# Four late modulation rows of a fused block: three of them summed in float32 on VectorE, one left as matrix-vector products on TensorE

## The chip, the cores and the metric

The kernel runs on one core of a Trainium2 chip. The metric is the device time of one execution in microseconds (us), the median of several runs. A core has TensorE (PE in the profile, with its weight loads as PEld), VectorE (DVE), ScalarE (ACT), GpSimd (POOL) and SyncE (SP), which here only starts transfers. In the profile, L12 is line 12 of the kernel.

## The reference

One transformer block with adaptive layer norm. A vector `c` gives six modulation rows of 1024 numbers; each scales, shifts or gates a part of the block.

```python
x = A_x                                            # (1, 2048, 1024), bfloat16
mod = (silu(c) @ w_mod).reshape(1, 6, 1, 1024)     # w_mod: 1024 x 6144
sa, ca, ga, sb, cb, gb = ...                       # the six rows
h = layernorm(x) * (1 + ca) + sa
x = x + ga * linear_attention(h, A_wqkv, A_wo)     # 32 heads of 32, phi(q), phi(k)
h = layernorm(x) * (1 + cb) + sb
x = x + gb * ((silu(h @ w_gate) * (h @ w_up)) @ w_down)   # 3584 hidden columns
```

`sa` and `ca` are needed at once. `ga`, `sb`, `cb` and `gb` are the four late rows that the change is about: `ga` multiplies the output weights `wo`, `sb` and `cb` shift and scale the second normalized rows, and `gb` gates the last output.

## The kernel before

The 2048 rows are worked in four chunks of 512 (`sc` 0 to 3). Of each chunk come the K groups, the V groups and the products K transposed times V; then the Q groups, numerators and denominators (`nd`), output products (`o`), the gate and up products (`GU`) and the down products (`D`). A group is eight matmuls into one of five PSUM banks that are used in turn. A list `seq` holds the matmul groups in order, and `put(label, ...)` hangs further work behind a group: each engine sees its instructions in exactly that order. Label ("V", 1, 3) is the fourth V group of chunk 1 ("V1.3" in the text).

The late rows as they are computed before: a block of 128 columns of `w_mod` is the stationary operand and one column of silu(c), `scT`, the moving one. So each result is a row turned onto the partitions, one number for each; eight products, one for each eighth of the 1024 inputs, add up in PSUM.

```python
LATE = [(2, "ga"), (3, "sb"), (4, "cb"), (5, "gb")]

def load_late(i):                      # half a row's columns of w_mod: 1 MB
    q, kb = LATE[i // 2][0], i % 2
    k0 = q * D + kb * NB
    nc.sync.dma_start(out=wml[i % 3], in_=wm_v[:, :, k0:k0 + NB])

def late_mm(i):                        # 32 products with one moving column
    ...
    for ii in range(NB // P):
        col = kb * (NB // P) + ii
        for j in range(DC):
            nc.tensor.matmul(mps[:, col:col + 1], lhsT=wml[i % 3][:, j, ii * P:(ii + 1) * P],
                             rhs=scT[:, j:j + 1], start=False, stop=(j == DC - 1), ...)
    if kb == 1:
        nc.vector.tensor_copy(out=m1[:, q, :], in_=mps[:, 0:DC])
```

`sb` and `cb` are used in that form (one number for each partition). `ga` and `gb` are needed along the free axis and alike on all partitions, so they are spread and transposed:

```python
def late_fin(q):
    ...                                # sb: copy; cb: add 1
        nc.vector.tensor_copy(out=rep[:], in_=m1[:, q, :].unsqueeze(2).to_broadcast([P, DC, P]))

def late_bc(q, dst):
    for h in range(NH):
        b = nextbank()
        for i in range(NB // P):
            cc = h * (NB // P) + i
            nc.tensor.matmul(b[:, i * P:(i + 1) * P], lhsT=rep[:, cc, :], rhs=ident[:], ...)
        nc.scalar.copy(out=dst[:, h * NB:(h + 1) * NB], in_=b[:])
```

The work of VectorE beside them in these stages: a K or Q group is evacuated by ScalarE (exp) and two VectorE operations, a V group by ScalarE alone. Behind every second K group stands the layer norm of 128 rows of the next chunk (`ln`): statistics on VectorE, then a power and two more operations on GpSimd, then a DMA transpose. In V4 and V6 of the stage the transposed rows are modulated on VectorE (`modulate`), and the next chunk's K groups need them.

```python
def phi_to(dst, acc):
    nc.scalar.activation(out=e[:], in_=acc, func=ACT.Exp)
    nc.vector.tensor_scalar(out=e[:], in0=e[:], scalar1=1.0, scalar2=PHI_EPS, op0=ALU.min, op1=ALU.add)
    nc.vector.scalar_tensor_tensor(out=dst, in0=acc, scalar=0.0, in1=e[:], op0=ALU.max, op1=ALU.add)

def modulate(sc_, cc, sT, c1T, c0=0, c1=SCW):
    h = M4[:, sc_, cc, c0:c1]
    nc.vector.tensor_scalar(out=h, in0=h, scalar1=c1T[:, cc:cc + 1], scalar2=sT[:, cc:cc + 1], ...)
```

The places of the late work before:

```python
put(("V", 0, 6), lambda: load_late(0), lambda: load_late(1), lambda: load_late(2))
lab = [(k, sc, i) for sc in (1, 2) for k in ("K", "V") for i in (2, 6)]
for i in range(8):
    put(lab[i], lambda i=i: late_mm(i))
    if i + 3 < 8:
        put(lab[i], lambda i=i: load_late(i + 3))
put(("K", 1, 7), lambda: late_fin(2))
put(("V", 1, 1), lambda: late_bc(2, ga_bc))
put(("V", 1, 7), lambda: late_fin(3))
put(("K", 2, 0), lambda: nc.sync.dma_start(out=wo, in_=wo_v))
put(("K", 2, 7), lambda: late_fin(4))
put(("V", 2, 7), lambda: late_fin(5))
put(("K", 3, 1), lambda: late_bc(5, gb_bc))
for cc in range(DC):
    put(("V", 3, cc), lambda cc=cc: nc.vector.tensor_tensor(out=wo[:, cc, :], in0=wo[:, cc, :], in1=ga_bc[:], ...))
```

At the start PE runs 21 products of a zero tile (`warm`) until the first normalized rows are there.

Of the kernel before, what the change touches and what calls it, by code (L numbers as in the profile page):

```python
# [9 lines left out]
ALU = mybir.AluOpType  # L10
BF16 = mybir.dt.bfloat16
F32 = mybir.dt.float32  # L12
# [9 lines left out]
def kernel(  # L22
# [13 lines left out]
    nc = tc.nc  # L36
    P = nc.NUM_PARTITIONS
    _, S, D = A_x.shape
# [3 lines left out]
    DC = D // P  # L42
# [5 lines left out]
    NB = 512  # L48
    NH = D // NB
# [13 lines left out]
    wo_v = A_wo.rearrange("(c p) n -> p c n", p=P)  # L63
# [3 lines left out]
    wm_v = w_mod.rearrange("(p j) n -> p j n", j=DC)  # L67
    c_v = c.rearrange("o (p j) -> p (o j)", j=DC)

    const = ctx.enter_context(tc.tile_pool(name="const", bufs=1))  # L70
# [6 lines left out]
    bank = [psum.tile([P, NB], F32, name=f"bank{i}") for i in range(8)]  # L77
# [3 lines left out]
    M3 = const.tile([P, 16384], BF16, name="M3")  # L81
    M4 = const.tile([P, NSC, DC, SCW], BF16, name="M4")
    M5 = const.tile([P, 14336], BF16, name="M5")
# [3 lines left out]
    def view(region, off, shape, dtype=BF16):  # L87
        n = 1
        for s_ in shape:
            n *= s_  # L90
        w = n * (2 if dtype == F32 else 1)
        ap = region[:, off:off + w]
        if dtype == F32:
            ap = ap.bitcast(F32)
        if len(shape) == 2:
            ap = ap.rearrange("p (a b) -> p a b", a=shape[0])
        elif len(shape) == 3:
            ap = ap.rearrange("p (a b c) -> p a b c", a=shape[0], b=shape[1])
        return ap
# [8 lines left out]
    wml = [view(M3, 4096 * (1 + i), [DC, NB]) for i in range(3)]  # L108
# [9 lines left out]
    wo = view(M6, 0, [DC, D])  # L118
    x1rs = [view(M6, 2048 * i, [D], F32) for i in range(2)]
    obs = [view(M6, 4096 + 1024 * i, [D]) for i in range(2)]  # L120
    yts = [view(M6, 6144 + 1024 * i, [NB], F32) for i in range(2)]
    xs = [view(M7, 1024 * i, [D]) for i in range(6)]
    xns = [view(M7, 6144 + 1024 * i, [D]) for i in range(6)]
    wgs = [view(M7, 4096 * i, [DC, FBW]) for i in range(3)]
# [11 lines left out]
    def load_x(st):  # L136
        nc.sync.dma_start(out=xs[st % 6], in_=x2[st * P:(st + 1) * P, :])
# [22 lines left out]
    load_wk(6, 7)  # L160
    load_wk(7, 8)

    zt = const.tile([P, NB], BF16, name="zt")
    nc.vector.memset(zt[:], 0.0)
    ident = const.tile([P, P], BF16, name="ident")
    make_identity(nc, ident[:])
    neg_half = const.tile([P, 1], F32, name="neg_half")
# [6 lines left out]
    sbT = const.tile([P, DC], BF16, name="sbT")  # L174
    cb1T = const.tile([P, DC], BF16, name="cb1T")
    m1 = const.tile([P, 6, DC], BF16, name="m1")
    ga_bc = const.tile([P, D], BF16, name="ga_bc")
    gb_bc = const.tile([P, D], BF16, name="gb_bc")
    KVZ = const.tile([P, HG, KVW], BF16, name="KVZ")
    rep = const.tile([P, DC, P], BF16, name="rep")  # L180

    scT = const.tile([P, DC], BF16, name="scT")
    nc.scalar.activation(out=scT[:], in_=c_sb[:], func=ACT.Silu)

    def warm(n):
        for _ in range(n):
            nc.tensor.matmul(bank[7][:], lhsT=zt[:, 0:P], rhs=zt[:], start=True, stop=True)


    stat = {}  # L190
# [39 lines left out]
    def nextbank():  # L230
        b = bank[state["b"]]
        state["b"] = (state["b"] + 1) % 5
        return b
# [51 lines left out]
                                    in1=mask[:, P:KVW].unsqueeze(1).to_broadcast([P, n, HPC]), op=ALU.mult)  # L285


    LATE = [(2, "ga"), (3, "sb"), (4, "cb"), (5, "gb")]

    def load_late(i):  # L290
        q, kb = LATE[i // 2][0], i % 2
        k0 = q * D + kb * NB
        nc.sync.dma_start(out=wml[i % 3], in_=wm_v[:, :, k0:k0 + NB])

    def late_mm(i):
        q, kb = LATE[i // 2][0], i % 2
        mps = bank[7][:, 320 + 8 * q:328 + 8 * q]
        for ii in range(NB // P):
            col = kb * (NB // P) + ii
            for j in range(DC):  # L300
                nc.tensor.matmul(mps[:, col:col + 1], lhsT=wml[i % 3][:, j, ii * P:(ii + 1) * P],  # L301
                                 rhs=scT[:, j:j + 1], start=False, stop=(j == DC - 1), skip_group_check=True)
        if kb == 1:
            nc.vector.tensor_copy(out=m1[:, q, :], in_=mps[:, 0:DC])

    def late_fin(q):
        if q == 3:
            nc.vector.tensor_copy(out=sbT[:], in_=m1[:, 3, :])
        elif q == 4:
            nc.vector.tensor_scalar_add(out=cb1T[:], in0=m1[:, 4, :], scalar1=1.0)  # L310
        else:
            nc.vector.tensor_copy(out=rep[:], in_=m1[:, q, :].unsqueeze(2).to_broadcast([P, DC, P]))

    def late_bc(q, dst):
        for h in range(NH):
            b = nextbank()
            for i in range(NB // P):
                cc = h * (NB // P) + i
                nc.tensor.matmul(b[:, i * P:(i + 1) * P], lhsT=rep[:, cc, :], rhs=ident[:], start=True, stop=True)
            nc.scalar.copy(out=dst[:, h * NB:(h + 1) * NB], in_=b[:])  # L320


    def tr0(st):
# [25 lines left out]
    def mod_pair(p):  # L349
        mod_mm(0, 2 * p, 2 * p + 2)  # L350
        mod_mm(1, 2 * p, 2 * p + 2)
        mod_rows(2 * p, 2 * p + 2)

    warm(21)
    for st in range(STC):
        ln_stats(st)
    mask = const.tile([P, KVW], BF16, name="mask")
# [6 lines left out]
    ln_xn(0, False)  # L364
    tr0(0)
    warm(3)
    ln_xn(1, False)
    tr0(1)
# [56 lines left out]
    def put(label, *fns):  # L425
        after.setdefault(label, []).extend(fns)
# [154 lines left out]
    for sc in (2, 3):  # L581
        put_ln(sc, [("K", sc - 1, 1), ("K", sc - 1, 3), ("K", sc - 1, 5), ("K", sc - 1, 7),
                    ("V", sc - 1, 4), ("V", sc - 1, 6)])
    put(("V", 0, 6), lambda: load_late(0), lambda: load_late(1), lambda: load_late(2))
    put(("V", 0, 7), lambda: [load_x(st) for st in range(8, 12)])
    put(("V", 1, 7), lambda: [load_x(st) for st in range(12, 16)])


    lab = [(k, sc, i) for sc in (1, 2) for k in ("K", "V") for i in (2, 6)]
    for i in range(8):  # L590
        put(lab[i], lambda i=i: late_mm(i))
        if i + 3 < 8:
            put(lab[i], lambda i=i: load_late(i + 3))
    put(("K", 1, 7), lambda: late_fin(2))
    put(("V", 1, 1), lambda: late_bc(2, ga_bc))
    put(("V", 1, 7), lambda: late_fin(3))
    put(("K", 2, 0), lambda: nc.sync.dma_start(out=wo, in_=wo_v))
    put(("K", 2, 7), lambda: late_fin(4))
    put(("V", 2, 7), lambda: late_fin(5))
    put(("K", 3, 1), lambda: late_bc(5, gb_bc))  # L600
    for cc in range(DC):
        put(("V", 3, cc), lambda cc=cc: nc.vector.tensor_tensor(out=wo[:, cc, :], in0=wo[:, cc, :], in1=ga_bc[:],
                                                               op=ALU.mult))


    put(("KV", 3, 1), kvz_build)
# [77 lines left out]
```

## Time and profile before

| | |
|---|---|
| device time, median of 3 runs | 847.81 us (846.98 to 849.0) |
| span of the profiled execution | 845.9 us |
| matrix-vector products of the late rows (L301) | 256, from 66.2 to 124.5 us |
| transposing products of the two broadcasts (L319) | 16, first 81.2, last 131.9 us |
| loads of late w_mod columns (L293) | 8 of 1 MB, median 7.4 us from issue to landing |
| load of `wo` (L597) | 1 of 2 MB, issued at 95.2 us, 12.7 us to landing |
| DMA transposes of the first norm (L220) | 12, 3.0 to 6.7 us to landing, median 3.2 |

A group line of the profile reads: source line, engine, operation, output <- inputs, shapes, count | busy us in total, mean ns of one | idle time of the engine just ahead of them, and what ended most of it. A timeline line reads: start in us, duration in us, engine, source line, operation, count, and in brackets the idle time ahead and its releaser. Matmuls are pipelined, so their durations overlap and differences of starts tell what a stream of them costs. The slices of the page divide the span into 40 equal parts of 21.1 us, each digit a tenth of busy time.

### The profile page before, as it was taken

How to read it: one execution, taken by the hardware profiler on the slowest of the kernel's cores; microseconds unless marked ns; L12 is line 12 of the kernel's file. 1: busy time of each engine (PE TensorE's matmuls, PEld its weight loads, DVE VectorE, ACT ScalarE, POOL GpSimd, SP SyncE). 2: the span in 40 equal slices, each digit the busy share in tenths (PEclk: the TensorE clock that was granted, in tenths of full speed). 3: DMA queues.
4: the chain of work that ended last, by engine and by line, in shares of the span. 5: the costliest groups of instructions: out<-in, count | busy, mean ns of one | idle time of the engine just before them, and what ended most of it. 6: DMA issues, size and time to landing. Idle time of an engine off the chain costs nothing.

```text
span 845.9 us, 10893 instructions
## 1 busy us (share of the span) xinstructions
PE 833.4 (99%) x4368; PEld 395.7 (47%) x4452; DVE 322.9 (38%) x617; ACT 144.8 (17%) x270; POOL 78.8 (9%) x142
## 2 busy tenths in 40 slices
PE   8999999999999999999999999999999999999998
PEld 4454554544444444444444444444444444444444
DVE  5667455488755655421111222211122122112222
ACT  4333223322211111111110001111000111100000
POOL 2124130013122323100000000000000000000000
PEclk9999999999999999999999999999999999999999
DMA  9995982056489888778875215555322555201220
GB/s 290 307 242 132 273 196 56 1 125 159 95 220 228 209 220 212 187 227 259 246 232 176 69 60 163 150 150 149 106 75 70 154 154 158 82 18 63 76 69 26
DMA packets 203763, 128.65 MB, mean 152 GB/s; under 512 B 50496, under 2 KB 189888, under 8 KB 203712
## 3 DMA queue, kind: packets, MB, share of 16 engines
q1 hardware_dynamic: 162864, 98.58, 41.0%
q10 hardware_dynamic: 38544, 20.98, 11.2%
q0 software_dynamic: 2304, 8.39, 2.6%
q8 instruction: 35, 0.57, 0.3%
q14 instruction: 16, 0.13, 0.0%
HBM read 103.81 MB, written 12.58 MB: 138 GB/s over the span
## 4 chain that ended last, share of the span: by engine, by line
PE 95%; DVE 1%; SPq 1%; DMA 1%; issue 1%; ACT 0%; DVEq 0%
PE bank L511 23%; PE bank L530 23%; PE bank L505 23%; PE bank L462 7%; PE bank L265 6%; PE bank L257 6%; PE bank L242 5%; DMA M<-in_w_mod_dram 1%; PE bank L435 1%; PE bank L274 1%; PE bank L301 1%; SPq L145 1%; SPq L142 1%; DVE stats L196 0%; DVE M L239 0%
## 5 line engine op out<-in xcount | busy, mean ns | idle before, releaser
L511 PE MATMUL bank<-M,M 128*128 128x512 bf16 x881 | 210.4, 379 | 0.8
L505 PE MATMUL bank<-M,M 128*128 128x512 bf16 x871 | 209.7, 379 | 1.3
L513 DVE TENSOR_TENSOR M<-bank,e 128x512 bf16<-128x512 f32 x112 | 77.4, 691 | 275.1 <-PE bank L511 265.7
L530 PE MATMUL bank<-M,M 128*128 128x512 bf16 (+1 forms) x687 | 146.9, 370 | 0.6
L508 ACT ACTIVATE e<-bank 128x512 f32<-128x512 f32 x112 | 66.8, 597 | 439.7 <-PE bank L505 415.7
L530 PEld LDWEIGHTS <-M 128*128 128x128 bf16 x924 | 90.4, 98 | 103.3
L511 PEld LDWEIGHTS <-M 128*128 128x128 bf16 x896 | 87.7, 98 | 105.7
L505 PEld LDWEIGHTS <-M 128*128 128x128 bf16 x896 | 87.3, 98 | 103.8
L534 DVE TENSOR_TENSOR M<-bank,gb_bc 128x512 f32<-128x512 f32 (+1 forms) x33 | 22.3, 675 | 149.2 <-PE bank L530 135.3
L242 PE MATMUL bank<-M,M 128*128 128x512 bf16 x244 | 57.3, 379 | 1.6 <-DVE M L224 0.6
L462 PE MATMUL bank<-M,M 128*128 128x512 bf16 x254 | 57.8, 379 | 0.1
L265 PE MATMUL bank<-M,M 128*128 128x512 bf16 x250 | 56.7, 379 | 0.3
L257 PE MATMUL bank<-M,M 128*128 128x512 bf16 x250 | 56.2, 379 | 0.3
L237 ACT ACTIVATE e<-bank 128x512 f32<-128x512 f32 x64 | 37.8, 598 | 101.9 <-PE bank L265 48.4
L530 PE MATMUL bank<-M 128*128 128x512 bf16 x219 | 50.7, 379 | 0.3
L239 DVE SCALAR_TENSOR_TENSOR M<-bank,e 128x512 bf16<-128x512 f32 x64 | 44.3, 692 | 3.7
L238 DVE TENSOR_SCALAR e<-e 128x512 f32<-128x512 f32 x64 | 27.7, 433 | 40.5 <-ACT e L237 40.5
L462 PEld LDWEIGHTS <-M 128*128 128x128 bf16 x256 | 25.0, 98 | 29.7
L257 PEld LDWEIGHTS <-M 128*128 128x128 bf16 x256 | 24.7, 98 | 29.0
L265 PEld LDWEIGHTS <-M 128*128 128x128 bf16 x256 | 24.6, 98 | 27.8
L242 PEld LDWEIGHTS <-M 128*128 128x128 bf16 x256 | 24.0, 97 | 28.8 <-DVE M L224 2.1
L464 DVE TENSOR_TENSOR M<-bank,M 128x512 f32<-128x512 f32 x32 | 22.1, 690 | 14.5 <-PE bank L462 14.3
(66 smaller groups left out, 334.1 us busy)
## 6 DMA issues: line engine op xcount, KB each, us to landing
M<-in_B_w_gate_dram SPq DMA_DIRECT2D x56, 512.0 KB, 3.9
M<-in_B_w_up_dram SPq DMA_DIRECT2D x56, 512.0 KB, 5.0
M<-in_w_mod_dram SPq DMA_DIRECT2D x8, 1024.0 KB, 7.4
x_scratch<-M POOLq DMA_DIRECT2D x16, 512.0 KB, 5.6
M<-x_scratch ACTq DMA_DIRECT2D x16, 512.0 KB, 3.4
M<-in_B_w_down_dram SPq DMA_DIRECT2D x6, 1024.0 KB, 7.9
M<-in_A_x_dram SPq DMA_DIRECT2D x16, 256.0 KB, 6.6
M<-in_w_mod_dram SPq DMA_DIRECT2D x8, 512.0 KB, 8.1
```

What stands on the lines that cost most here:

```text
L237: nc.scalar.activation(out=e[:], in_=acc, func=ACT.Exp)
L238: nc.vector.tensor_scalar(out=e[:], in0=e[:], scalar1=1.0, scalar2=PHI_EPS, op0=ALU.min, op1=ALU.add)
L239: nc.vector.scalar_tensor_tensor(out=dst, in0=acc, scalar=0.0, in1=e[:], op0=ALU.max, op1=ALU.add)
L242: nc.tensor.matmul(acc[:], lhsT=M4[:, sc_, cc, t * P:(t + 1) * P], rhs=wk[:, cc, h * NB:(h + 1) * NB], start=(cc == 0), stop=(cc == DC - 1))
L257: nc.tensor.matmul(acc[:], lhsT=M4[:, sc_, cc, t * P:(t + 1) * P], rhs=wv[:, cc, h * NB:(h + 1) * NB], start=(cc == 0), stop=(cc == DC - 1))
L265: nc.tensor.matmul(acc[:], lhsT=wq[:, cc, qc * P:(qc + 1) * P], rhs=M4[:, sc_, cc, :], start=(cc == 0), stop=(cc == DC - 1))
L462: nc.tensor.matmul(acc[:], lhsT=oTs[st % 3][:, cc, :], rhs=wo[:, cc, hs], start=(cc == 0), stop=(cc == DC - 1))
L505: nc.tensor.matmul(g_ps[:], lhsT=wg_blk[:, cc, fs], rhs=M4[:, sc_, cc, :], start=(cc == 0), stop=(cc == DC - 1))
L508: nc.scalar.activation(out=sg[:], in_=g_ps[:], func=ACT.Silu)
L511: nc.tensor.matmul(u_ps[:], lhsT=wu_blk[:, cc, fs], rhs=M4[:, sc_, cc, :], start=(cc == 0), stop=(cc == DC - 1))
L513: nc.vector.tensor_tensor(out=gus[sc_][:, f, :], in0=u_ps[:], in1=sg[:], op=ALU.mult)
L530: nc.tensor.matmul(y_ps[:, 0:w], lhsT=gus[sc_][:, f, t * P:(t + 1) * P], rhs=wd(f)[:, c0:c1], start=(f == 0), stop=(f == FC - 1))
```

## The change

Three of the four late rows leave the matrix-vector form. Each partition holds eight rows of `w_mod`; VectorE multiplies them with the partition's eight values of silu(c) and adds them in float32, which leaves 128 partial rows. A product with ones on PE adds the 128 partitions: with a matrix of ones as the stationary operand the sum comes out alike on all partitions (`ga`, `gb`), with the partial row as the stationary operand and one column of ones as the moving one it comes out turned onto the partitions (`sb`). [...]the float32 sum is split into a high part and a rest, and both are multiplied. `cb` stays in the matrix-vector form. The aim is to take matrix-vector products from TensorE and to use VectorE where it idles; `sb` and `gb` are computed later than before (`gb` in the second chunk's gate and up stage), and the multiplication of `wo` by `ga` moves from the V groups of the last chunk to its K groups.

```diff
+    accA = view(M5, 8256, [D], F32)
+    hlA = [view(M5, 10304 + 1024 * i, [2, NB]) for i in range(2)]
+    accG = view(M3, 12288, [D], F32)
+    hlG = view(M3, 14336, [2, NB])
 ...
-    zt = const.tile([P, NB], BF16, name="zt")
+    zt = view(M5, 13376, [NB])
-    rep = const.tile([P, DC, P], BF16, name="rep")
+    ones = const.tile([P, P], BF16, name="ones")
+    nc.gpsimd.memset(ones[:], 1.0)
+    scF = const.tile([P, DC], F32, name="scF")
 ...
+    nc.scalar.copy(out=scF[:], in_=scT[:])
 ...
+    def late_sum(acc, kb, slot, js):
+        dst = acc[:, kb * NB:(kb + 1) * NB]
+        for j in js:
+            if j == 0:
+                nc.vector.tensor_scalar_mul(out=dst, in0=wml[slot][:, 0, :], scalar1=scF[:, 0:1])
+            else:
+                nc.vector.scalar_tensor_tensor(out=dst, in0=wml[slot][:, j, :], scalar=scF[:, j:j + 1], in1=dst,
+                                         op0=ALU.mult, op1=ALU.add)
+
+    def late_split(acc, kb, hl):
+        src = acc[:, kb * NB:(kb + 1) * NB]
+        nc.vector.tensor_copy(out=hl[:, 0, :], in_=src)
+        nc.vector.tensor_tensor(out=hl[:, 1, :], in0=src, in1=hl[:, 0, :], op=ALU.subtract)
+
+    def late_cols(q, kb, hl):
+        o = 320 + 8 * q
+        for ii in range(NB // P):
+            col = o + kb * (NB // P) + ii
+            for s_ in range(2):
+                nc.tensor.matmul(bank[7][:, col:col + 1], lhsT=hl[:, s_, ii * P:(ii + 1) * P], rhs=ones[:, 0:1], ...)
+
+    def late_vec(q, kb, slot):          # as late_mm before, for cb
 ...
-    def late_bc(q, dst):
-        for h in range(NH):
-            b = nextbank()
-            for i in range(NB // P):
-                cc = h * (NB // P) + i
-                nc.tensor.matmul(b[:, i * P:(i + 1) * P], lhsT=rep[:, cc, :], rhs=ident[:], start=True, stop=True)
-            nc.scalar.copy(out=dst[:, h * NB:(h + 1) * NB], in_=b[:])
+    def late_bc(kb, hl, dst):
+        b = nextbank()
+        for s_ in range(2):
+            nc.tensor.matmul(b[:], lhsT=ones[:], rhs=hl[:, s_, :], start=(s_ == 0), stop=(s_ == 1))
+        nc.scalar.copy(out=dst[:, kb * NB:(kb + 1) * NB], in_=b[:])
 ...
-    warm(21)
+    warm(17)
 ...
+    def sums(acc, kb, slot, labels):
+        for i, lab in enumerate(labels):
+            put(lab, lambda i=i: late_sum(acc, kb, slot, (2 * i, 2 * i + 1)))
+
+    put(("V", 0, 6), lambda: load_late(CB, 0, 0), lambda: load_late(CB, 1, 1), lambda: load_late(GA, 0, 2))
+    put(("K", 1, 2), lambda: late_vec(CB, 0, 0), lambda: load_late(GA, 1, 0))
+    put(("K", 1, 6), lambda: late_vec(CB, 1, 1), lambda: load_late(SB, 0, 1))
+    put(("V", 1, 7), lambda: late_fin(CB))
+    sums(accA, 0, 2, [("V", 1, k) for k in range(4)])
+    put(("V", 1, 3), lambda: late_split(accA, 0, hlA[0]), lambda: load_late(SB, 1, 2))
+    put(("K", 2, 2), lambda: late_bc(0, hlA[0], ga_bc))
+    put(("K", 2, 3), lambda: nc.sync.dma_start(out=wo, in_=wo_v))
+    sums(accA, 1, 0, [("V", 2, k) for k in range(4)])
+    put(("V", 2, 3), lambda: late_split(accA, 1, hlA[1]))
+    put(("K", 3, 0), lambda: late_bc(1, hlA[1], ga_bc))
+    for kb in range(2):
+        sums(accA, kb, 1 + kb, [("V", 3, 4 * kb + k) for k in range(4)])
+    put(("V", 3, 4), lambda: late_split(accA, 0, hlA[0]))
+    put(("KV", 3, 0), lambda: late_split(accA, 1, hlA[1]))
+    put(("Q", 1, 2), lambda: late_cols(SB, 0, hlA[0]), lambda: late_cols(SB, 1, hlA[1]), lambda: late_fin(SB))
+    put(("GU", 0, 20), lambda: load_late(GB, 0, 0), lambda: load_late(GB, 1, 1))
+    for kb in range(2):
+        sums(accG, kb, kb, [("GU", 1, 5 * kb + i) for i in range(4)])
+        put(("GU", 1, 5 * kb + 4), lambda kb=kb: late_split(accG, kb, hlG))
+        put(("GU", 1, 5 * kb + 6), lambda kb=kb: late_bc(kb, hlG, gb_bc))
     for cc in range(DC):
-        put(("V", 3, cc), lambda cc=cc: nc.vector.tensor_tensor(out=wo[:, cc, :], in0=wo[:, cc, :], in1=ga_bc[:], ...))
+        put(("K", 3, 2 + cc) if cc < 6 else ("V", 3, cc - 6), lambda cc=cc: ...)    # the same product
```

The sums of V1.0 and on are hung behind V groups, so they stand in VectorE's order behind the last layer norm of the K stage and ahead of the modulation.

More of the change, by code (lines that the diff above doesn't have):

```diff
@@ L161 @@
     load_wk(7, 8)
-    zt = const.tile([P, NB], BF16, name="zt")
-    nc.vector.memset(zt[:], 0.0)
+    zt = view(M5, 13376, [NB])
+    nc.vector.memset(zt, 0.0)
     ident = const.tile([P, P], BF16, name="ident")
@@ L179 @@
     KVZ = const.tile([P, HG, KVW], BF16, name="KVZ")
-    rep = const.tile([P, DC, P], BF16, name="rep")
+    ones = const.tile([P, P], BF16, name="ones")
+    nc.gpsimd.memset(ones[:], 1.0)
+    scF = const.tile([P, DC], F32, name="scF")
     scT = const.tile([P, DC], BF16, name="scT")
     nc.scalar.activation(out=scT[:], in_=c_sb[:], func=ACT.Silu)
+    nc.scalar.copy(out=scF[:], in_=scT[:])
     def warm(n):
         for _ in range(n):
-            nc.tensor.matmul(bank[7][:], lhsT=zt[:, 0:P], rhs=zt[:], start=True, stop=True)
+            nc.tensor.matmul(bank[7][:], lhsT=zt[:, 0:P], rhs=zt, start=True, stop=True)
     stat = {}
@@ L285, in kvz_build, with load_late @@
                                     in1=mask[:, P:KVW].unsqueeze(1).to_broadcast([P, n, HPC]), op=ALU.mult)
-    LATE = [(2, "ga"), (3, "sb"), (4, "cb"), (5, "gb")]
-    def load_late(i):
-        q, kb = LATE[i // 2][0], i % 2
+    GA, SB, CB, GB = 2, 3, 4, 5
+    def load_late(q, kb, slot):
         k0 = q * D + kb * NB
-        nc.sync.dma_start(out=wml[i % 3], in_=wm_v[:, :, k0:k0 + NB])
-    def late_mm(i):
-        q, kb = LATE[i // 2][0], i % 2
-        mps = bank[7][:, 320 + 8 * q:328 + 8 * q]
[L298 to L310, printed above, removed]
-        else:
-            nc.vector.tensor_copy(out=rep[:], in_=m1[:, q, :].unsqueeze(2).to_broadcast([P, DC, P]))
-    def late_bc(q, dst):
-        for h in range(NH):
-            b = nextbank()
-            for i in range(NB // P):
-                cc = h * (NB // P) + i
-                nc.tensor.matmul(b[:, i * P:(i + 1) * P], lhsT=rep[:, cc, :], rhs=ident[:], start=True, stop=True)
-            nc.scalar.copy(out=dst[:, h * NB:(h + 1) * NB], in_=b[:])
+        nc.sync.dma_start(out=wml[slot], in_=wm_v[:, :, k0:k0 + NB])
@@ new lines, in late_cols @@
+    def late_cols(q, kb, hl):
[3 more added lines that the diff above has]
+            for s_ in range(2):
+                nc.tensor.matmul(bank[7][:, col:col + 1], lhsT=hl[:, s_, ii * P:(ii + 1) * P], rhs=ones[:, 0:1],
+                                 start=False, stop=(s_ == 1), skip_group_check=True)
+    def late_vec(q, kb, slot):
+        o = 320 + 8 * q
+        for ii in range(NB // P):
+            col = o + kb * (NB // P) + ii
+            for j in range(DC):
+                nc.tensor.matmul(bank[7][:, col:col + 1], lhsT=wml[slot][:, j, ii * P:(ii + 1) * P],
+                                 rhs=scT[:, j:j + 1], start=False, stop=(j == DC - 1), skip_group_check=True)
@@ new lines, in late_fin @@
+    def late_fin(q):
+        mps = bank[7][:, 320 + 8 * q:328 + 8 * q]
+        if q == SB:
+            nc.vector.tensor_copy(out=sbT[:], in_=mps)
+        else:
+            nc.vector.tensor_copy(out=m1[:, q, :], in_=mps)
+            nc.vector.tensor_scalar_add(out=cb1T[:], in0=m1[:, q, :], scalar1=1.0)
+    def late_bc(kb, hl, dst):
[3 more added lines that the diff above has]
+        nc.scalar.copy(out=dst[:, kb * NB:(kb + 1) * NB], in_=b[:])
@@ L583 @@
                     ("V", sc - 1, 4), ("V", sc - 1, 6)])
-    put(("V", 0, 6), lambda: load_late(0), lambda: load_late(1), lambda: load_late(2))
     put(("V", 0, 7), lambda: [load_x(st) for st in range(8, 12)])
     put(("V", 1, 7), lambda: [load_x(st) for st in range(12, 16)])
[L589 to L600, printed above, removed]
+    def sums(acc, kb, slot, labels):
+        for i, lab in enumerate(labels):
+            put(lab, lambda i=i: late_sum(acc, kb, slot, (2 * i, 2 * i + 1)))
+    put(("V", 0, 6), lambda: load_late(CB, 0, 0), lambda: load_late(CB, 1, 1), lambda: load_late(GA, 0, 2))
@@ L601 @@
+    for kb in range(2):
+        sums(accG, kb, kb, [("GU", 1, 5 * kb + i) for i in range(4)])
+        put(("GU", 1, 5 * kb + 4), lambda kb=kb: late_split(accG, kb, hlG))
+        put(("GU", 1, 5 * kb + 6), lambda kb=kb: late_bc(kb, hlG, gb_bc))
     for cc in range(DC):
-        put(("V", 3, cc), lambda cc=cc: nc.vector.tensor_tensor(out=wo[:, cc, :], in0=wo[:, cc, :], in1=ga_bc[:],
-                                                               op=ALU.mult))
+        put(("K", 3, 2 + cc) if cc < 6 else ("V", 3, cc - 6),
+            lambda cc=cc: nc.vector.tensor_tensor(out=wo[:, cc, :], in0=wo[:, cc, :], in1=ga_bc[:], op=ALU.mult))
```

## The prediction

> **What bounds the kernel now.** I read the page's busy shares first, then its slices.
>
> ```profile
> PE 833.4 (99%) x4368; PEld 395.7 (47%) x4452; DVE 322.9 (38%) x617; ACT 144.8 (17%) x270; POOL 78.8 (9%) x142
> ...
> PE   8999999999999999999999999999999999999998
> ...
> DVE  5667455488755655421111222211122122112222
> ```
>
> TensorE (PE) is busy in every slice, and the chain of work that ended last is 95% PE. So the time falls only where PE has fewer instructions, or where PE waited. VectorE (DVE) is the engine with room, though not in slices 5 to 12 (about 65 to 190 us), which is where most of the new work goes. Next, the groups by shape: what the change removes (L301, L319) and what resembles the work it adds to VectorE.
>
> ```profile
> L239 DVE SCALAR_TENSOR_TENSOR M<-bank,e 128x512 bf16<-128x512 f32 x64 | 44.3, 692 | 3.7
> ...
> L238 DVE TENSOR_SCALAR e<-e 128x512 f32<-128x512 f32 x64 | 27.7, 433 | 40.5 <-ACT e L237 40.5
> ...
> L301 PE MATMUL bank<-scT,M 128*128 128x1 bf16 x256 | 7.5, 163 | 0.1
> ...
> L319 PE MATMUL bank<-ident,rep 128*128 128x128 bf16 x16 | 1.2, 220 | 1.0 <-DVE rep L312 1.0
> ```
>
> The mean of 163 ns is the latency of one, not what it costs in a pipelined stream. For the cost I take differences of starts in PE's timeline around the first broadcast:
>
> ```profile
> 76.62 3.62 PE L257 MATMUL bank<-M,M 128*128 128x512 bf16 x16
> 81.22 0.62 PE L319 MATMUL bank<-ident,rep 128*128 128x128 bf16 x8 [0.98 <-DVE rep L312]
> 81.68 1.89 PE L257 MATMUL bank<-M,M 128*128 128x512 bf16 x8
> 83.41 0.94 PE L301 MATMUL bank<-scT,M 128*128 128x1 bf16 x32
> 84.21 7.07 PE L257 MATMUL bank<-M,M 128*128 128x512 bf16 x31
> ```
>
> Eight 512-wide products take 83.41 - 81.68 = 1.73 us, 0.216 each. A block of 32 matrix-vector products takes 84.21 - 83.41 = 0.80 us, 25 ns each. Eight transposing products of the broadcast take 81.68 - 81.22 = 0.46 us. The sixteen products from 76.62 should have ended issuing at 76.62 + 16 x 0.216 = 80.07, so PE stood 1.15 us for `rep`. Last, where VectorE idles in the K and V stages:
>
> ```profile
> 80.48 0.68 DVE L312 COPY rep<-m 128x1024 bf16<-128x1024 bf16 x1
> 90.06 2.67 DVE L224 TENSOR_SCALAR M<-M,ca1T,saT 128x512 bf16<-128x512 bf16 x8 [8.89 <-DMA M<-M]
> ...
> 114.73 0.16 DVE L310 TENSOR_SCALAR cb1T<-m 128x8 bf16<-128x8 bf16 x1
> 120.41 2.68 DVE L224 TENSOR_SCALAR M<-M,ca1T,saT 128x512 bf16<-128x512 bf16 x8 [5.52 <-DMA M<-M]
> ...
> 144.26 4.89 DVE L602 TENSOR_TENSOR M<-M,ga_bc 128x1024 bf16<-128x1024 bf16 x8
> 159.63 0.43 DVE L238 TENSOR_SCALAR e<-e 128x512 f32<-128x512 f32 x1 [10.48 <-ACT e L237]
> ```
>
> The holes are 8.89 us in V1, 5.52 us in V2 and 10.48 us in V3. The first two end when the transposed rows of the next chunk land, and then the modulation (L224) must run, because PE needs it at once for K2 and K3.
>
> **What the Trainium skill says.** "TensorE: Matmul & The Clock Gate", section "Wait — 56ns, not 53.3ns?", gives a floor of about 25 ns between starts however narrow the product, and 215.7 ns for 512 columns; the trace agrees (25 and 216). "VectorE: DVE Perf Modes", section "The TRN2 errata", has (N+151)/0.96 for a float32 sum of two tensors, 691 ns at N=512; the trace shows 690 to 692 for L464, L513 and L535. "SBUF — State Buffer", section "SBUF: two separate sides", says that a VectorE operation with two SBUF inputs and a GpSimd operation that reads SBUF lock each other out for a whole instruction. The kernel before has few such pairs; a trace of something like it is the GpSimd power at 80.65, which took 0.92 us beside the copy to `rep` where its median is about 0.6.
>
> **The change part by part: TensorE.**
> - Removed: six of eight late blocks, 6 x 0.80 = 4.8 us. Only `cb` keeps its two.
> - Removed: both transposing broadcasts, 2 x 0.46 = 0.9 us, and the first one's wait, 1.15 us (the second shows none).
> - Added: 16 one-column products for `sb`, 16 x 0.025 = 0.4 us.
> - Added: four broadcasts with ones, two 512-wide products each, 8 x 0.216 = 1.73 us.
> - Sum: -4.8 - 0.9 - 1.15 + 0.4 + 1.73 = -4.7 us.
> - The four warm-up products less (some 0.9 us at the end of the warm-up) I count as nothing. The transposes that follow wait for ScalarE's normalized rows, and PE later waits for w_mod to land at 19.5 and 21.3 us, which does not move.
>
> **VectorE.** Each half row is one scaling (0.43, as L238), seven dependent multiply-adds (0.69 each), a copy (0.43, my guess of the form) and a subtraction (0.69). A dependent instruction starts 0.03 us after its forerunner's end (L238 at 60.31 for 0.43, L239 at 60.77), so a half row takes 0.46 + 7 x 0.72 + 0.46 + 0.69 = 6.65 us, and six of them 40 us. They displace nothing if they lie in holes:
> - V1: the work of K1 ends at 80.5, the sums at 87.1, before the 90.06 at which the modulation started: free.
> - V2: PE has gained by then and reaches K2 3.2 us earlier (1.15 + 0.46 + two blocks), so VectorE ends its K2 work at about 111.3 and the sums at 118.0. The modulation then takes 2.7 us, to 120.7.
> - V3: the products of `wo` move into K3 (0.61 us each beside 1.07 for the evacuation of a group, under 1.73 of PE), two remaining; 13.3 + 1.2 us of work in the 15.4 us that were the old products plus the hole. Just free.
> - The `gb` row: 2 multiply-adds in each 3.46 us of the up and gate stage, where VectorE is a fifth busy: free. Its 2 MB load comes at some 328 us, eight column steps of 3.46 us before it is used.
>
> **Rivals, and what each would make of the time.**
> - A new wait of PE at the start of K2 and K3 replaces part of the gain. PE would be at K3 at 127.19 - 3.2 - 3.2 (four blocks) + 0.43 = 121.2 us and need the eighth modulated piece 1.5 us later, at 122.7. The last rows leave GpSimd at 117.11 - 3.5 = 113.6, or about 1.3 later if its three operations are each held by a multiply-add with two SBUF inputs. The transposes land 3.2 us (median) to 6.7 us (longest) after issue, and the 2 MB of `wo`, now loaded in K2 instead of ahead of it, can make it the longer one: 118 to 121.6, the modulation ends at 120.8 to 124.3, PE waits 0 to 1.6 us. At K2 the same sum gives 0 to 0.8. For it: the locks and the displaced `wo` load. Against it: the late w_mod load that competed with the transposes at 84.6 us now comes after the sums. I take 0.15 at K2 and 0.6 at K3. At its worst: 845.5 us.
> - VectorE becomes the bound in V3, late for the K,V mask and the first numerators. For it: the hole is filled to within 1 us. Against it: PE reads the masked product 2.6 us after VectorE made it, and five rotating banks carry evacuations. Cost up to 1 us; 844.8 at most with the first rival as taken.
> - The gain was hidden anyway, PE meeting a DMA later. Against it: after 22 us PE has no DMA wait in its groups. This would give 847; I do not believe it.
> - The `gb` load delays weights of the next blocks. Between 325 and 345 us the DMA moved about 190 GB/s where it reaches 380 elsewhere, and weights are issued some 19 us ahead. Near zero.
>
> **The range and the chances.** 847.81 - 4.7 + 0.75 = 843.86, given as 843.8 us. The three runs before lie 2 us apart, so the median of a few runs is good to about 1 us. With no new wait it is 843.1, less 1 for scatter: 842.0. With the worst waits and scatter: 846.0. 2% are 17 us, more than the whole of what is removed or added on PE, so both outer chances are 0.01.
>
> **What would show each step.** PE's busy time falls by 3.5 to 4 us, and the blocks of 32 occur twice, not eight times, in K1. The wait of PE on `rep` is gone. Multiply-adds read near 690 ns, and the six half rows near 6.7 us each. The VectorE holes in V1, V2 and V3 shrink to under 3 us; those in GU stay. A PE idle on L224 ahead of K2 or K3 sizes the first rival. I am wrong if multiply-adds are much slower beside GpSimd, if a PE wait above 2 us appears in the K, V or Q stages, or if PE waits for weights after 328 us.

## The result and the profile after

| | before | after |
|---|---|---|
| device time, median | 847.47 us (846.98 to 849.0, 4 runs) | 842.53 us (842.26 to 842.78, 4 runs) |
| span of the profiled execution | 845.9 us | 840.4 us |

The ratio is 0.9939, with a 95% interval of 0.9921 to 0.9956: 4.9 us less. Both medians are of few runs. In the comparisons of the experiments below the kernel before has 847.24 to 847.33 us (9 to 27 runs), and the kernel after, run again, 842.74 us: about 4.6 us less. In the kernel after, L250 are the K groups, L265 the V groups, L282 the products K transposed times V, L329 the products left to `cb`, L343 the broadcasts with ones, L321 the one-column products for `sb`, L306 and L308 the scaling and the multiply-adds of the sums, L313 and L314 the split, L232 the modulation.

First the busy shares and VectorE's slices, in the form of the page of before.

```profile
PE 827.8 (99%) x4182; PEld 390.6 (46%) x4264; DVE 361.5 (43%) x672; ACT 145.1 (17%) x271; POOL 79.8 (10%) x143
...
DVE  5768779988655655354111221111212111112222
```

VectorE carries 38.6 us more, and its slices 4 to 7 (the first counted as 0; 85 to 169 us) rise from 4, 5, 5, 4 to 7, 7, 9, 9. PE is still busy everywhere. Its fall of 5.6 us should not be read as the gain, though. Some 80 matmuls have no record in either profile (4368 of 4452 have one before, 4182 of 4264 after), and experiment 5, with the same 4264 matmuls and all of them recorded, has 834.2 us. And 2.3 us of the fall are the products of the zero tile, of which three stand behind the warm-up itself: 24 are busy for 8.3 us before and 20 for 6.0 us after. Differences of starts do not suffer from missing records, so the comparison rests on them. PE's timeline of the kernel after in the K and V stages:

```profile
75.72 13.98 PE L265 MATMUL bank<-M,M 128*128 128x512 bf16 x63
89.53 1.07 PE L282 MATMUL bank<-M 128*128 128x129 bf16 x16
90.44 1.89 PE L250 MATMUL bank<-M,M 128*128 128x512 bf16 x8
92.17 1.07 PE L282 MATMUL bank<-M 128*128 128x129 bf16 x16
93.29 3.40 PE L250 MATMUL bank<-M,M 128*128 128x512 bf16 x15
96.53 0.59 PE L343 MATMUL bank<-M,ones 128*128 128x512 bf16 x2
96.96 8.80 PE L250 MATMUL bank<-M,M 128*128 128x512 bf16 x39
...
120.31 1.89 PE L250 MATMUL bank<-M,M 128*128 128x512 bf16 x8
122.04 0.59 PE L343 MATMUL bank<-M,ones 128*128 128x512 bf16 x2
```

The V stage of chunk 1 is one unbroken stretch: no block of 32, no wait for `rep`. The two products with ones take 96.96 - 96.53 = 0.43 us. At 120.31 us K3 begins, without a wait. And what VectorE does in the hole of V1, and in that of V2:

```profile
79.58 0.48 DVE L306 TENSOR_SCALAR M<-M,scF 128x512 f32<-128x512 bf16 x1
80.09 6.29 DVE L308 SCALAR_TENSOR_TENSOR M<-M,scF,M 128x512 f32<-128x512 bf16 x7
86.42 0.43 DVE L313 CAST M<-M 128x512 bf16<-128x512 f32 x1
86.88 0.69 DVE L314 TENSOR_TENSOR M<-M 128x512 bf16<-128x512 f32 x1
87.49 2.67 DVE L232 TENSOR_SCALAR M<-M,ca1T,saT 128x512 bf16<-128x512 bf16 x8
...
117.63 0.69 DVE L314 TENSOR_TENSOR M<-M 128x512 bf16<-128x512 f32 x1
118.84 2.67 DVE L232 TENSOR_SCALAR M<-M,ca1T,saT 128x512 bf16<-128x512 bf16 x8 [0.52 <-DMA M<-M]
```

The sums of V1 fill 79.58 to 87.49 us, and the modulation follows without a wait for the transposes. In V2 it still waits 0.52 us for them.

To compare kernels step by step I count from the first V group of chunk 0, because the time up to there differs from execution to execution by itself (experiments 1 and 2). Its first product starts at 31.77 us before and at 30.86 us after.

| PE's distance from the first V group (us) | before | after | difference | by the prediction's terms |
|---|---|---|---|---|
| K2 begins | 94.55 - 31.77 = 62.78 | 90.44 - 30.86 = 59.58 | -3.20 | -3.2 |
| K3 begins | 127.19 - 31.77 = 95.42 | 120.31 - 30.86 = 89.45 | -5.97 | -6.0 |
| first Q group of chunk 1 begins | 157.08 - 31.77 = 125.31 | 150.19 - 30.86 = 119.33 | -5.98 | -6.0 |
| first numerators begin | 164.89 - 31.77 = 133.12 | 158.40 - 30.86 = 127.54 | -5.58 | -5.6 |
| end of the span | 845.9 - 31.77 = 814.1 | 840.4 - 30.86 = 809.5 | -4.6 | -4.7 |

The last column adds up the prediction's terms for what stands ahead of each point. The profiles of the kernel after and of experiments 1 and 8, which differ from it by nothing or by the warm-up alone, agree in the last row within 0.1 us; the kernel before and experiment 2 have 814.1 and 814.5, so there 0.4 us are not read. The gain is largest at K3, where all blocks of 32 that fall away have passed. The sixteen products for `sb` give 0.4 us back ahead of the numerators, and `gb`'s two broadcasts the rest, in the second chunk's gate and up stage.

### The profile page after: what moved, and what is told of

Read it like the earlier page. It is cut to its first block, busy times and chain, and to the rows that moved or that the text cites. A ratio compares the mean times of both kernels' runs of the same rounds, so it can differ in the third digit from the quotient of the medians.

```text
span 840.4 us, 10575 instructions
## 1 busy us (share of the span) xinstructions
PE 827.8 (99%) x4182; PEld 390.6 (46%) x4264; DVE 361.5 (43%) x672; ACT 145.1 (17%) x271; POOL 79.8 (10%) x143
## 4 chain that ended last, share of the span: by engine, by line
PE 97%; SPq 1%; DMA 1%; issue 1%; DVE 0%
PE bank L554 23%; PE bank L535 23%; PE bank L529 23%; PE bank L486 7%; PE bank L265 7%; PE bank L273 7%; PE bank L250 6%; DMA M<-in_w_mod_dram 1%; PE bank L459 1%; PE bank L282 1%; SPq L149 1%; SPq L146 0%; PE bank L343 0%; PE bank L329 0%; SPq L141 0%
## 5 line engine op out<-in xcount | busy, mean ns | idle before, releaser
L250 PE MATMUL bank<-M,M 128*128 128x512 bf16 x245 | 56.7, 379 | 1.5 <-DVE M L232 0.6
L265 PE MATMUL bank<-M,M 128*128 128x512 bf16 x252 | 55.7, 379 | 0.2
L247 DVE SCALAR_TENSOR_TENSOR M<-bank,e 128x512 bf16<-128x512 f32 x64 | 44.3, 691 | 3.9
L265 PEld LDWEIGHTS <-M 128*128 128x128 bf16 x256 | 25.1, 98 | 30.2
L250 PEld LDWEIGHTS <-M 128*128 128x128 bf16 x256 | 24.2, 98 | 29.5 <-DVE M L232 2.1
```

Source lines behind the costliest of these rows:

```text
L250: nc.tensor.matmul(acc[:], lhsT=M4[:, sc_, cc, t * P:(t + 1) * P], rhs=wk[:, cc, h * NB:(h + 1) * NB], start=(cc == 0), stop=(cc == DC - 1))
L265: nc.tensor.matmul(acc[:], lhsT=M4[:, sc_, cc, t * P:(t + 1) * P], rhs=wv[:, cc, h * NB:(h + 1) * NB], start=(cc == 0), stop=(cc == DC - 1))
```

## The experiments

Theory A is the prediction's: the gain is the sum of what PE no longer issues or waits for, less what it issues in its place, and VectorE's work is free because it stands in holes. The rivals are the warm-up (B), relief of VectorE or other waits (C), a gain that is hidden again (D), sums that delay the layer norm or the modulation (E), VectorE having room anywhere (F), and the place of the `wo` load (G).

| | device time, median (us) | first V group (us) | span (us) | rest of the span (us) |
|---|---|---|---|---|
| before | 847.47 | 31.77 | 845.9 | 814.1 |
| after | 842.53 | 30.86 | 840.4 | 809.5 |
| 1 after, 21 warm-up products | 842.78 | 31.19 | 840.7 | 809.5 |
| 2 before, 17 warm-up products | 847.78 | 31.03 | 845.5 | 814.5 |
| 3 before, broadcast of ga later | 846.08 | 31.43 | 844.5 | 813.1 |
| 4 after, sb as vectors | 844.10 | 31.48 | 842.2 | 810.7 |
| 5 after, no multiply-adds | 842.50 | 31.36 | 840.9 | 809.5 |
| 6 after, sums in K2 | 845.91 | 31.36 | 844.1 | 812.7 |
| 7 after, high part only | 841.85 | 31.60 | 840.1 | 808.5 |
| 8 after, again | 842.74 | 32.89 | 842.4 | 809.5 |
| 9 high part only, wo load early | 841.75 | 31.45 | 839.9 | 808.5 |

**1 and 2: the warm-up.**

```diff
-    warm(17)
+    warm(21)
```

> The changed kernel with 21 instead of 17 warm-up products at the start, nothing else. In the profile of the change PE stands 0.9 us earlier than before when the V groups of chunk 0 begin (30.86 against 31.93 us), which the prediction counted as nothing. Theory A (the start is set by the landing of w_mod, which differs from run to run): device time unchanged within 0.5 us of 842.5, and the wait for w_mod takes up the 0.9 us. Theory B (the shorter warm-up gives it): 0.9 us longer, about 843.4, and PE 0.9 us later at the V groups of chunk 0.

```diff
-    warm(21)
+    warm(17)
```

> The kernel before with 17 instead of 21 warm-up products, nothing else. Theory A (landing of w_mod sets the start): unchanged within 0.5 us. Theory B (the warm-up counts): 0.9 us shorter, V groups of chunk 0 at about 31.0 instead of 31.9 us.

Measured: 842.78 us for the kernel after with 21 products. The kernel before with 17 has 847.78 us against 847.24 for before beside it, a ratio of 1.0006 (0.9998 to 1.0014): not shorter. So four warm-up products are worth nothing that can be measured here, and B is out. In its profile experiment 2 does start the V groups at 31.03 us, as B says, but the other profiles show that this is chance. (The 31.93 us of the expectation should read 31.77.) In nine of the eleven profiles of the table PE waits for `w_mod` ahead of a block of 16 products of the early rows, and in eight of them, all but experiment 8, the first V group follows the start of that block by 10.5 to 10.6 us. It starts at 20.29 us after, at 20.65 in experiment 1, at 20.48 in experiment 2 and at 21.27 before. These four alone could pass for an order by the number of warm-up products. All eight do not: 20.29 to 21.05 us with 17 products, 20.65 to 21.27 with 21. In experiments 5 and 6 this wait is missing, and the first V group starts at 31.36 us all the same.

**3: the wait for rep alone.**

```diff
-    put(("V", 1, 1), lambda: late_bc(2, ga_bc))
+    put(("V", 1, 5), lambda: late_bc(2, ga_bc))
```

> The kernel before with the broadcast of ga hung behind the sixth V group of chunk 1 instead of the second, so that rep is long ready. Theory A (the gain is a sum: PE instructions plus the 1.15 us in which PE stood for rep): 1.15 us shorter, no wait of PE on rep in the profile, 846.3 against 847.5. Rival C (the gain of the change is mostly that VectorE no longer holds PE in the K and V stages): 3 us or more shorter. Rival D (the wait was made up for later): unchanged.

Measured: 846.08 us against 847.24 for before beside it, ratio 0.9991 (0.9983 to 0.9999); from the first V group on 1.1 us less. PE's timeline where the broadcast now stands:

```profile
82.49 5.13 PE L257 MATMUL bank<-M,M 128*128 128x512 bf16 x23
87.45 0.61 PE L319 MATMUL bank<-ident,rep 128*128 128x128 bf16 x8
87.90 1.89 PE L257 MATMUL bank<-M,M 128*128 128x512 bf16 x8
```

No bracket stands behind L319: the wait is gone, and with it 1.1 us to the end of the kernel. The interval of the ratio (0.1 to 1.4 us) is wide, but PE's distance to K3 is shorter by 1.15 us as well: 125.70 - 31.43 = 94.27 against 95.42. So a quarter of the change's gain was to be had by moving one line, with no sums at all. Neither rival C (3 us or more) nor D (nothing) fits.

**4: one row put back.**

```diff
-    for kb in range(2):
-        sums(accA, kb, 1 + kb, [("V", 3, 4 * kb + k) for k in range(4)])
-    put(("V", 3, 4), lambda: late_split(accA, 0, hlA[0]))
-    put(("KV", 3, 0), lambda: late_split(accA, 1, hlA[1]))
-    put(("Q", 1, 2), lambda: late_cols(SB, 0, hlA[0]), lambda: late_cols(SB, 1, hlA[1]), lambda: late_fin(SB))
+    put(("V", 3, 2), lambda: late_vec(SB, 0, 1))
+    put(("V", 3, 6), lambda: late_vec(SB, 1, 2))
+    put(("Q", 1, 2), lambda: late_fin(SB))
```

> The changed kernel with the row sb back in the form before: 64 matrix-vector products behind V3.2 and V3.6, no sums, split or products with ones for it. Theory A (each product with one column costs PE 25 ns wherever it stands): 48 more products, 48 x 0.025 = 1.2 us longer, 843.7, PE busy rises by as much. Rival C (most of the gain is relief of VectorE and waits): shorter or unchanged, because VectorE loses 13 us of work in V3.

Measured: 844.10 us, and 1.2 us more than the kernel after from the first V group on. PE's timeline of V3:

```profile
141.26 0.94 PE L329 MATMUL bank<-scT,M 128*128 128x1 bf16 x32
142.07 7.07 PE L265 MATMUL bank<-M,M 128*128 128x512 bf16 x31
148.97 0.94 PE L329 MATMUL bank<-scT,M 128*128 128x1 bf16 x32
149.78 1.89 PE L265 MATMUL bank<-M,M 128*128 128x512 bf16 x7
```

Each block costs 0.81 us again (142.07 - 141.26, 149.78 - 148.97), though VectorE has 13 us less to do beside it. 2 x 0.81 - 0.4 = 1.2. That is A to a tenth of a microsecond, and the opposite of C.

**5: the sums left out.** Each half row is made from its first eighth alone.

```diff
             else:
-                nc.vector.scalar_tensor_tensor(out=dst, in0=wml[slot][:, j, :], scalar=scF[:, j:j + 1], in1=dst,
-                                         op0=ALU.mult, op1=ALU.add)
+                pass
```

> The changed kernel without its 42 multiply-adds: each half row keeps the scaling of its first eighth, the split and the products with ones, so three rows are made from an eighth of their inputs and the output is not the reference's. It asks what the sums on VectorE cost. Theory A (they lie in holes): unchanged within 0.5 us, 842.5, while VectorE's busy time falls by some 33 us. Rival E (they delay the layer norm or the modulation, through GpSimd's lock or VectorE's order): shorter by 1 us or more.

Measured: 842.50 us, and from the first V group on the same 809.5 us. The busy shares:

```profile
PE 834.2 (99%) x4264; PEld 391.2 (47%) x4264; DVE 330.5 (39%) x630; ACT 145.0 (17%) x271; POOL 79.5 (9%) x143
```

VectorE has 31.0 us less and the time does not move: in the places where the change puts them, 42 multiply-adds cost nothing. E is out as a cost, though its mechanism is there: in V1 the modulation starts 1.4 us earlier without the multiply-adds (86.60 - 31.36 against 87.49 - 30.86). PE does not notice. In the kernel after the modulation of V1 ends at 87.49 + 2.67 = 90.16 us, and PE needs its last piece at 90.44 + 7 x 0.216 = 91.95.

**6: the same sums in another place.**

```diff
-    sums(accA, 1, 0, [("V", 2, k) for k in range(4)])
-    put(("V", 2, 3), lambda: late_split(accA, 1, hlA[1]))
+    sums(accA, 1, 0, [("K", 2, 2 * k + 1) for k in range(4)])
+    put(("K", 2, 7), lambda: late_split(accA, 1, hlA[1]))
```

> The changed kernel with the sums of ga's second half hung behind K2.1, K2.3, K2.5 and K2.7 (the split behind K2.7) instead of V2.0 to V2.3: the same work, but where VectorE has no idle time. Theory A (the sums are free only because they stand in holes): VectorE ends K2 some 5 us later, the last rows reach their transposes and the modulation that much later, and PE waits for the modulation ahead of K3: 3 to 6 us longer, with a wait of PE on the modulation line. Rival F (43% busy VectorE has room anywhere): unchanged.

Measured: 845.91 us, 3.2 us more than the kernel after from the first V group on; two thirds of the gain are lost. PE's timeline shows two new waits:

```profile
113.22 8.79 PE L265 MATMUL bank<-M,M 128*128 128x512 bf16 x40 [1.79 <-DVE M L247]
121.85 1.07 PE L282 MATMUL bank<-M 128*128 128x129 bf16 x16
123.29 2.65 PE L250 MATMUL bank<-M,M 128*128 128x512 bf16 x8 [0.36 <-DVE M L232]
```

The first is not the one that I expected: in V2 PE waits 1.79 us for a PSUM bank, because VectorE is behind with the evacuations of K2 (L247) and only five banks rotate. At K3 it waits 0.36 us for the modulation, and then the eight products that follow take 2.65 us where they take 1.89 in the kernel after, as each waits for its piece. By PE's starts, counted from the first V group, the products K transposed times V behind V2 begin 1.95 us later than in the kernel after (121.85 - 31.36 against 119.40 - 30.86), K3 another 0.53 later, and the eight products take 0.75 more (125.77 - 123.29 against 122.04 - 120.31). Together that is the whole 3.2 us. VectorE's timeline at that point:

```profile
118.43 1.57 DVE L314 TENSOR_TENSOR M<-M 128x512 bf16<-128x512 f32 x1
122.82 2.67 DVE L232 TENSOR_SCALAR M<-M,ca1T,saT 128x512 bf16<-128x512 bf16 x8 [2.82 <-DMA M<-M]
```

Counted from the first V group, the modulation starts 3.5 us later than in the kernel after (122.82 - 31.36 against 118.84 - 30.86). VectorE itself then waits 2.82 us for the transposes: the layer norm of the last rows, which comes behind the sums in its order, was late. F is out. The average load does not tell: VectorE is busy for 43% of the span in both kernels, and the sums cost 0 us in V2 and 3.2 us in K2.

**7 and 9: the high part alone, and the place of the wo load.** The partial sums are rounded to bfloat16 once, and the rest is left out; in 9 the load of `wo` also goes back to K2.0. Experiment 8 is the kernel after, unchanged, beside 9 on one chip.

```diff
-        nc.vector.tensor_tensor(out=hl[:, 1, :], in0=src, in1=hl[:, 0, :], op=ALU.subtract)
 ...
-            for s_ in range(2):
-                nc.tensor.matmul(bank[7][:, col:col + 1], lhsT=hl[:, s_, ii * P:(ii + 1) * P], rhs=ones[:, 0:1], ...)
+            nc.tensor.matmul(bank[7][:, col:col + 1], lhsT=hl[:, 0, ii * P:(ii + 1) * P], rhs=ones[:, 0:1], ...)
 ...
-        for s_ in range(2):
-            nc.tensor.matmul(b[:], lhsT=ones[:], rhs=hl[:, s_, :], start=(s_ == 0), stop=(s_ == 1))
+        nc.tensor.matmul(b[:], lhsT=ones[:], rhs=hl[:, 0, :], start=True, stop=True)
```

> The changed kernel without the low part of the split: the float32 sums are rounded to bfloat16 once, one product with ones instead of two, no subtraction. Theory A: 4 x 0.216 + 8 x 0.025 = 1.06 us less on PE, 841.5. Rival E: more than that, about 2 us, if the subtraction (0.69 us on VectorE in each half row) stood in the way of the modulation. Rival D (hidden by another wait): unchanged.

```diff
-    put(("K", 2, 3), lambda: nc.sync.dma_start(out=wo, in_=wo_v))
+    put(("K", 2, 0), lambda: nc.sync.dma_start(out=wo, in_=wo_v))
```

> The changed kernel as it is, beside the next one on the same chip, so that a difference of one us can be read. All theories: 842.5 within 0.5 us; the start of the V groups of chunk 0 anywhere between 30.8 and 32.0 us.

> The changed kernel with the high part of the sums alone, and with the load of wo back behind K2.0 (before: K2.0, changed: K2.3). Theory A (PE instructions are all that counts, the transposes ahead of K3 have just room enough): 1.06 us less than the changed kernel on the same chip, as with the high part alone; the wait of VectorE for the transposed rows ahead of K3 (0.5 us in the changed kernel) goes, without worth to PE. Rival G (the wo load in front of the transposes costs PE time at K3): another 0.5 us or more less.

Measured: 841.85 us for 7, ratio 0.9933 (0.9921 to 0.9946) to before. For 9 it is 841.75 us, beside 842.74 us for the kernel after: 1.0 us less, and from the first V group on both 7 and 9 have 808.5 against 809.5. That is A's 1.06 us and not the 2 us of E, and these versions are faster than both kernels. G is out: VectorE's timeline ahead of K3, first of experiment 7, then of 9:

```profile
117.91 0.43 DVE L313 CAST M<-M 128x512 bf16<-128x512 f32 x1
119.67 2.68 DVE L232 TENSOR_SCALAR M<-M,ca1T,saT 128x512 bf16<-128x512 bf16 x8 [1.33 <-DMA M<-M]
```

```profile
117.74 0.43 DVE L313 CAST M<-M 128x512 bf16<-128x512 f32 x1
118.08 2.67 DVE L232 TENSOR_SCALAR M<-M,ca1T,saT 128x512 bf16<-128x512 bf16 x8
```

With `wo` loaded earlier the modulation follows the copy at once; with `wo` in front of the transposes it waits 1.33 us, and the slowest transpose takes 8.7 us to land instead of 4.8. The rest of the span differs by less than 0.1 us, so the wait hardly reaches PE: the eight products at the start of K3 take 1.79 us in 7 and 1.73 in 9. Experiment 8 missed its range for the start: its first V group is at 32.89 us, not between 30.8 and 32.0 (see the last section). What follows it takes 809.5 us, as it should.

## Why the prediction was right

843.8 us was predicted (842.0 to 846.0), 842.53 us measured: a gain of 4.0 us against 4.9, or against 4.6 by the longer series of runs and by the distances. The mechanism held, not only the number: the gain is what PE no longer issues or waits for.

- **The sum on PE held.** -4.7 us was worked out and -4.6 us is what the distances show, and each term can be found in the table above or in an experiment: 0.80 us for a block (0.81 in experiment 4), 1.15 us for the wait (1.1 in experiment 3), 0.43 us for a broadcast with ones, 0.4 us for the sixteen products.
- **The warm-up at nothing held** (experiments 1 and 2), as far as these runs can tell.
- **VectorE's work free in the holes held** (experiment 5), though one term was too small. A half row was put at 6.65 us; it takes 87.49 - 79.58 = 7.9 us in V1. The multiply-add was taken from a sum of two tensors (0.69 us) and takes 0.75. And in V1 and V2 one of the seven takes 1.57 us, because GpSimd's normalization runs beside it. GpSimd's timeline in V1:

```profile
79.75 0.72 POOL L210 TENSOR_TENSOR rstd<-veps,neg_half 128x1 f32<-128x1 f32 x1 [1.50 <-DVE veps L208]
80.56 0.42 POOL L212 TENSOR_SCALAR nmr<-mv,rstd 128x1 f32<-128x1 f32 x1
81.08 1.62 POOL L219 TENSOR_SCALAR M<-M,rstd,nmr 128x1024 bf16<-128x1024 bf16 x1
```

The last operation takes 1.62 us, where its counterpart at 82.04 us before, beside an idle VectorE, took 1.19; in experiment 5, without the multiply-adds, it takes 1.19 too. This agrees with what the Trainium skill says in "SBUF — State Buffer", section "SBUF: two separate sides": a VectorE operation with two SBUF inputs and a GpSimd operation that reads SBUF exclude each other. The prediction allowed 1.3 us of delay for the three operations; in V2 they need 113.44 - 110.49 = 2.95 us where they needed 117.11 - 114.90 = 2.21, so 0.7 more. That delay is not the multiply-adds' alone: in experiment 5, where the copy and the subtraction of the split stand in their place, the three need 115.12 - 112.19 = 2.93 us.

- **VectorE did not become the bound in V3.** The sums fill the hole there: from 127.66 to 157.10 us VectorE has no idle time that the profile shows. The masked K, V products are ready at 155.57 us, and PE reads them at 158.40, 2.8 us later, where the prediction had 2.6 for the kernel before. The table shows no loss there, only the 0.4 us of the products for `sb`.
- **The rival of a new wait was mis-sized: 0.75 us taken, none measured.** In the kernel after no wait of PE stands ahead of K2 or K3. Ahead of K3 the mechanism is there. The transposes end VectorE's wait at 118.84 us, at the early end of the 118 to 121.6 that was given (though the slowest transpose of the kernel after takes 8.6 us to land, more than the 6.7 that the range allowed), and the modulation ends at 121.51. PE needs the eighth piece at 120.31 + 7 x 0.216 = 121.8. So 0.3 us were left; experiment 6 shows what it costs when they are used up. This term and the starting point make up most of the 1.3 us between 843.8 and 842.53: 847.81, the median of three runs, was 0.3 us above the 847.47 of four and 0.5 above the 847.24 to 847.33 of the longer series.
- **The load of gb cost PE nothing**, as taken. The DMA does fill (273 to 333 GB/s between 330 and 345 us, against 58 to 288 before), but the 0.8 and 1.1 us of PE idle ahead of the gate and up products are no more than before (0.8 and 1.3).
- **One of the signs named was a poor one.** "PE's busy time falls by 3.5 to 4 us": it fell by 5.6 us, 2.3 of them in the warm-up, which is worth nothing to the time, and both profiles lack some 80 matmuls.

## What to carry to other kernels

When one engine is busy all the time, as PE is here, a change is worth the instructions that it takes off that engine, at their spacing in the stream (25 ns here, not the 163 ns of one), plus the waits that fall away. Work moved to another engine was free in a hole and not elsewhere: the same sums cost 0 us behind V groups and 3.2 us behind K groups, at the same average load. How near the edge a hole is has to be computed: ahead of K3 0.3 us were left. And look first for a wait that moving a single line removes; here it was a quarter of the gain.

## What the runs showed of the hardware that was not expected

A multiply-add on VectorE of a bfloat16 tensor, a scalar for each partition and a float32 tensor, 128x512 to float32, takes 0.75 us, and 1.57 us when a GpSimd operation is in its way. A subtraction of two tensors of that size takes 0.69 us, and 1.57 us beside GpSimd in experiment 6.

In the profiled execution of experiment 8 PE's clock fell to half during the start, after two waits for `w_mod` (0.46 us of weight loads, then 1.24 us). The busy times by stretch show it in the column PEclk, the one before DMA share and GB/s:

```profile
18.00:21.00 3.00, 1.76 (x26) 0.86 (x24) 0.00 (x0) 0.00 (x0) 0.00 (x0) 1.00 1.12 334
21.00:23.00 2.00, 2.00 (x21) 0.92 (x22) 1.10 (x5) 0.00 (x0) 0.00 (x0) 0.70 1.19 293
23.00:25.00 2.00, 1.78 (x5) 0.70 (x5) 0.00 (x0) 0.00 (x0) 0.00 (x0) 0.50 1.08 330
```

Five products in the two microseconds from 23 us, and a first V group at 32.89 us instead of 30.86 to 31.77; this execution took 844.29 us, where the median is 842.74. The kernel before had a like pair of waits in its profile (0.47 and 1.22 us) and kept the full clock, so why it fell here stays open.
